# Partition sums with bfloat16 ones, norms of x moved beside projections, and the last sum of x split, in a kernel that mixes a memory attention and a gated feed-forward

## The chip, the cores and the metric

The kernel runs on one core of a Trainium2 chip. The metric is the device time of one execution in microseconds. Engines are named as in the profile: PE is TensorE (PEld its weight loads), DVE is VectorE, ACT is ScalarE, POOL is GpSimd, SP is SyncE, which here issues the DMAs.

## The reference, cut to what matters

With S = 2048 tokens, D = 576, 32 heads of 18, F = 4608, and the tokens in N = 4 segments of L = 512:

```python
g = sigmoid((x * gate_w).sum(-1, keepdims=True))
q, k, v = x @ wq, x @ wk, x @ wv          # split in 32 heads and 4 segments
for s in range(4):                        # M, z: memory of the segments before
    p = softmax(q[s] @ k[s].T * scale + causal mask)
    a_dot = p @ v[s]
    a_mem = (phi(q[s]) @ M) / (phi(q[s]) @ z + 1e-6)
    o[s] = gb * a_mem + (1 - gb) * a_dot  # gb = sigmoid(beta), one for each head
    M += phi(k[s]).T @ v[s]; z += phi(k[s]).sum()
a = o @ wo
b = (gelu(x @ w_gate) * (x @ w_up)) @ w_down
return g * a + (1 - g) * b
```

`phi(t)` is t + 1 for t > 0, and exp(t) otherwise. All arrays are float32.

## The kernel before

Every large product is made in float16 pairs: a float32 operand is scaled by a power of two and split into a high and a low float16 word, and three products (high by high, high by low, low by high) are added in PSUM. The scales come from norms. A norm is a sum of squares, made along the free dimension by ACT or DVE into a column of `wst` or `stat`, and then over the 128 partitions by `sums` (L88): a product of a 128x128 matrix of ones with the few columns (3 to 10), whose result every partition holds. Only the exponent of the result is kept (`root`, `scale_of`, `scales`), so a scale is a power of two.

The work stands in an order written out by hand: inside `tc.manual_schedule` each of PE, ACT, DVE and POOL executes its instructions in the order in which the Python code issues them. An instruction that has to wait holds up all that stands behind it on its engine. PSUM has eight banks, given out by tag: `st` and `dn` (two each), `G`, `U`, `V` and `pv`. A new use of a bank waits until its last readers are done. `spare()` hands out `dn` or `V` in turns.

The stages:

- Segments s = 0 to 3 of 512 tokens. For s > 0, first the rows, q = 0 to 3: values for 128 tokens (`vrows`), transposes of the key rows of the segment before (`key_rows`, into G or st, and the last two into V), their product into the memory (`memorize`) and reads of the memory (`recall`). Then the projections j = 0 to 8 (`project`), each 14 products of 512 columns; a block of 128 columns of q or k goes to `put_columns`, which ACT and DVE work on: first words and an exponential on ACT, and later (`later`, `finish_later`) phi and the second words on DVE, an addition on POOL. What else belongs beside a projection is issued by `beside_products`, what belongs beside rows by `beside_rows` and `behind_rows`. The next segment's x is loaded, squared (`square_x`), added up over its five parts (`add_squares`) and split in words (`high_x`, `low_x`) beside the projections of the one before.
- `norm_x(c, o)` takes the added squares of segment c and multiplies them by ones over the partitions, 512 columns into bank V; DVE then takes the largest column as a bound for the hidden scales (`x2`). `NORMS` says where: beside the rows (1, 1), (1, 3), (2, 3) and (3, 0), ahead of `key_rows`.
- The feed-forward, `step(v)` for v = 0 to 71, two steps for each of 36 blocks of 128 hidden columns; a step handles two segments by Strassen-like sums of x and of the weights (`product`, `rest`, banks V, G, U). From the fifth step on a head of the attention is worked on beside it (`scores`, `powers`, `pair_rows`, `turn_rows`, `values`, `normalize`), and the product with `w_down` of the blocks before (`chains`, `down`, into banks dn by turns, added up by DVE at L1112). `scales` is called once in every four steps.
- `last_sum(p, i)` forms the last of the sums of two segments' x. For p = 1 it has three parts: a subtraction on POOL (i = 0, in segment 3), a copy that makes the high words on ACT, and a subtraction on DVE that makes the low words; the latter two with i = 1 in step 0, behind the first copy of G into U. Its result, the words of `x16[3]`, is first read in step 1.
- At the end the product with `wo`, and the stores.

Of the kernel before, what the change touches and what calls it, by code (L numbers as in the profile page):

```python
# [8 lines left out]
F32 = mybir.dt.float32  # L9
BF16 = mybir.dt.bfloat16  # L10
F16 = mybir.dt.float16
I32 = mybir.dt.int32
AF = mybir.ActivationFunctionType
# [5 lines left out]
P = 128  # L19
# [24 lines left out]
def kernel(ctx: ExitStack, tc: tile.TileContext, xs, wqk, wv, wo, wgu, wd, beta, out):  # L44
    nc = tc.nc
    pe, act, dve, pool, sp = nc.tensor, nc.scalar, nc.vector, nc.gpsimd, nc.sync

    cst = ctx.enter_context(tc.tile_pool(name="cst", bufs=1))
# [4 lines left out]
    def bank(tag, bufs=1, dt=F32):  # L53
        return ps.tile([P, 512 if dt == F32 else 1024], dt, name=tag, tag=tag, bufs=bufs)
# [11 lines left out]
    def flat(ap):  # L66
        return ap.rearrange("p a b -> p (a b)") if len(ap.shape) == 3 else ap
# [20 lines left out]
    def sums(st, o=None):  # L88

        o = (spare() if o is None else o)[:, : st.shape[1]]  # L90
        pe.matmul(o, ones, st, start=True, stop=True)
        return o

    def scale_of(i, total):
# [67 lines left out]
    def norm_x(c, o):  # L162
        pe.matmul(o, onesb, x_sq.pop(c)[:, :L], start=True, stop=True)
        n = x2[:, c : c + 1]
        dve.tensor_reduce(n, o, AX.X, OP.max)
        dve.tensor_scalar(n, n, 1e-30, None, OP.max)
# [209 lines left out]
    def last_sum(p, i):  # L376
        r, x, sc = sums_x[p], x16[2 * p + 1], xsc[:, 2 * p : 2 * p + 1]
        if i == 0:
            pool.tensor_tensor(r[2, 1], r[2, 1], r[2, 2], OP.subtract)
            return  # L380
        act.activation(flat(x[:, 0:2]), r[2, 1], AF.Copy, scale=sc)
        dve.scalar_tensor_tensor(flat(x[:, 4:6]), r[2, 1], sc, flat(x[:, 0:2]), OP.mult, OP.subtract)

    qks, vps, oms, oas = [], [], [], []
# [3 lines left out]
        oms.append(dram.tile([HT, D], F32, name="om"))  # L388
        oas.append(dram.tile([HT, 9 * P], F16, name="oa"))

    ones = cst.tile([P, P], F32, name="ones")
    onesb = cst.tile([P, P], BF16, name="onesb")
    mask = cst.tile([P, L], BF16, name="mask")
    gh = cst.tile([P, 2, H], F32, name="gh")
# [17 lines left out]
    with tc.tile_pool(name="prj", bufs=2, side="right", reuse_waits="tile") as pp:  # L412
# [44 lines left out]
        def make_v(k):  # L457
            t = W[9 + k] = pa.tile([P, 2, D + 2], F16, name="wv", bufs=5)
            pair_of(t, raw_v[:, k], wsc[:, 1:2])
# [201 lines left out]

        FIRST = (0,)
        with tc.manual_schedule(engines=ORDERED):
            pool.memset(onesb, 1.0)
            pool.memset(ones, 1.0)

            start = bank("G")
            for _ in range(30):
# [116 lines left out]
            def beside_products(s, j):  # L785
                if s < 3 and j == (4 if s else 5):
                    scale_x(s + 1, bank("V") if s == 0 else None)
                if s == 0:
                    if j == 0:
                        put_rows(0, 0, 0, va[0], usc, 1.0)  # L790
                        make_qk(3, pair_high)
                        finish_later()
                        make_qk(3, pair_low)
                    if j == 1:
                        scale_sum(0, wst[:, 10:19], va[3][:, 420:])
                        turns.update(of=3, n=4)
                        dve.tensor_scalar(unq, wis[:, 4:5], 2.0**-14, wsc[:, 0:1], OP.mult, OP.mult)
                        outscale(0, 0)
                        outscale(0, 2)
                        put_rows(0, 1, 0, va[1], usc, 1.0)  # L800
                        finish_later()
                    if j == 2:
                        make_qk(4)
                        make_v(1)
                        for q in (2, 3):
                            put_rows(0, q, 0, va[q], usc, 1.0)
                        for q in FIRST:
                            put_rows(0, q, 1, vb[q], usc, 1.0)
                        finish_later()
                        x_raw.pop(0)  # L810
                    if j == 3:
                        outscale(0, 1)
                    if j == 1 or 3 <= j < 6:
                        make_v(j - 1)
                if s == 1:
                    if j == 2:
                        dve.tensor_scalar(gh[:, 1], gh[:, 1], 1.0, None, OP.add)
                        dve.reciprocal(gh[:, 0], gh[:, 1])
                        dve.tensor_scalar(gh[:, 1], gh[:, 0], -1.0, 1.0, OP.mult, OP.add)
                    if j == 5:  # L820
                        for c in range(3):
                            mix_scale(c)
                if s < 3:
                    next_x(s + 1, j)
                if s == 2:
                    if j == 0:
                        form_sums(0, 2, 1)
                        last_sum(0, 0)
                    if j == 1:
                        last_sum(0, 1)  # L830
                    if j == 3:
                        load_sums(1)
                    if j == 8:
                        for f in range(3):
                            load_g(f)
                if s == 3:
                    if j == 0:
                        sums_g(0)
                        last_sum(1, 0)
                    if j == 1:  # L840
                        high_g(0, 1)
                        low_g(0, 1)
                    if j == 2:
                        load_d(0)
                        load_d(1)
                    if j == 4:
                        load_g(3)
                    if j == 6:
                        high_g(1, 0)
                        low_g(1, 0)  # L850
                        sums_g(1)
                        squares(1, 2, 0)
                        squares(1, 2, 1)
                    if j == 7:
                        squares(1, 3, 0, act_square)
                        squares(1, 0, 2, act_square)
                    if j == 8:
                        high_g(1, 1)
                        low_g(1, 1)
                        squares(1, 3, 1, act_square)  # L860
                        squares(1, 1, 2, act_square)
                    if 1 <= j < 4:
                        form_sums(1, j - 1, 2)
                    if 2 <= j < 5:
                        form_sums(1, j - 2, 1)

            NORMS = {(1, 1): (0,), (1, 3): (1,), (2, 3): (2,), (3, 0): (3,)}
            done = None
            for s in range(4):
                p = s - 1  # L870
                if s:
                    for q in range(4):
                        pv = vrows(s, q, 0)
                        if q == 0:
                            key_scale(p)
                        if done:
                            put_columns(*done)
                            done = None
                        finish_later()
                        put_rows(s, q, 0, *pv)  # L880
                        for c in NORMS.get((s, q), ()):
                            norm_x(c, bank("V"))
                        if q:
                            key_rows(p, q - 1)
                        beside_rows(s, q)
                        finish_later()
                        if held:
                            held.pop()()
                        behind_rows(s, q)
                        pv = vrows(s, q, 1)  # L890
                        put_rows(s, q, 1, *pv)
                        if p >= 1:
                            recall(p, q)
                        if q:
                            memorize(p, q - 1)
                    finish_later()
                    key_rows(p, 3)
                for j in range(9):
# [32 lines left out]
                    if s == 0 and j >= 6:  # L931
                        q = j - 5
# [20 lines left out]
    with tc.tile_pool(name="keep", bufs=2, side="right", reuse_waits="tile") as kp, ExitStack() as tail:  # L953
# [179 lines left out]
        def gelu(f, c, o, t):  # L1133
            act.activation(t, o, AF.Gelu_apprx_tanh, scale=scl[f // 2][0][:, 2 + c : 3 + c])  # L1134
# [94 lines left out]
        def step(v):  # L1229

            f, p = divmod(v, 2)
            fb, i4 = divmod(v, 4)
            c, e = 2 * p, 2 * p + 1
# [15 lines left out]
            V, g1 = ahead.pop(v) if v in ahead else first_product(v)  # L1249
# [1 line left out]
            product(X, f, A11, x1, 0, 4, True)  # L1251
            put(2 * k - 1, 3)
            dve.tensor_copy(Y, X)
            if v == 0:
                last_sum(1, 1)
            if v == 1:
                scale_result()
            if v != 4:
# [31 lines left out]
            if not fb:  # L1290
                dve.tensor_tensor(g0, V, g0, OP.add)
                gelu(f, c, g0, g0)
            some(fb - 1, early[0 if v == 4 else 1 : 2])
            if v == 2 * NF - 1:
                finish(2)
# [18 lines left out]
            put(2 * k, 1)  # L1314
            dve.tensor_tensor(g1, Y, g1, OP.add)  # L1315
            gelu(f, e, g1, g1)
            if v == 3:
                for n in range(2):
                    high_d(n)
                    low_d(n)  # L1320
# [303 lines left out]
```

## Time and profile before

| | |
|---|---|
| median of 3 runs | 1573.54 us (1573.29 to 1574.6) |
| profiled execution, own time | 1574.6 us |
| its span, first to last instruction | 1572.9 us |
| granted TensorE clock, mean | 0.999 |
| busy: PE, DVE, ACT, POOL | 1563.1, 1150.6, 1174.8, 1232.8 us |
| DMA | 209.90 MB, 133 GB/s |

A busy time is the sum of an engine's instructions; PE's matmuls are pipelined, so that one's duration runs on beside the start of the next. In the order of time a row is a start, a duration, engine, line, operation, output and inputs with their shapes, a count of merged instructions, and in brackets the idle time ahead of it with what ended it.

### The profile page before, as it was taken

How to read it: one execution, taken by the hardware profiler on the slowest of the kernel's cores; microseconds unless marked ns; L12 is line 12 of the kernel's file. 1: busy time of each engine (PE TensorE's matmuls, PEld its weight loads, DVE VectorE, ACT ScalarE, POOL GpSimd, SP SyncE). 2: the span in 40 equal slices, each digit the busy share in tenths (PEclk: the TensorE clock that was granted, in tenths of full speed). 3: DMA queues.
4: the chain of work that ended last, by engine and by line, in shares of the span. 5: the costliest groups of instructions: out<-in, count | busy, mean ns of one | idle time of the engine just before them, and what ended most of it. 6: DMA issues, size and time to landing. Idle time of an engine off the chain costs nothing.

```text
span 1572.9 us, 32770 instructions
## 1 busy us (share of the span) xinstructions
PE 1563.1 (99%) x11920; PEld 927.9 (59%) x11920; DVE 1150.6 (73%) x3027; ACT 1174.8 (75%) x1999; POOL 1232.8 (78%) x1184
## 2 busy tenths in 40 slices
PE   9999999999999999999999999999999999999998
PEld 5665754555555555555555555555555555555576
DVE  6788975767777776767777777777676777776565
ACT  7566544988788888878888878888887888885421
POOL 4354765888888879898888888887979788888697
PEclk9999999999999999999999999999999999999999
DMA  6633332688888799988888889888798978784644
GB/s 233 211 125 112 136 122 69 118 125 128 136 132 142 123 151 128 139 127 137 130 128 131 136 133 140 138 129 155 127 134 137 137 135 130 130 132 83 142 107 130
DMA packets 472826, 209.90 MB, mean 133 GB/s; under 512 B 427688, under 2 KB 437416, under 8 KB 472152
## 3 DMA queue, kind: packets, MB, share of 16 engines
q1 hardware_dynamic: 472664, 207.80, 73.4%
q8 instruction: 94, 1.54, 0.4%
q14 instruction: 68, 0.56, 0.1%
HBM read 91.87 MB, written 27.26 MB: 76 GB/s over the span
## 4 chain that ended last, share of the span: by engine, by line
PE 94%; ACT 2%; DVE 1%; POOL 1%; issue 1%; DMA 0%; SPq 0%; POOLq 0%; ACTq 0%; DVEq 0%
PE dn L1104 27%; PE U L1144 18%; PE V L1144 12%; PE G L1144 12%; PE pv L1059 4%; PE dn L342 2%; PE st L335 2%; PE U L1151 2%; PE V L1156 1%; PE G L1156 1%; PE st L1012 1%; PE st L1464 1%; PE V L1151 1%; PE G L1151 1%; PE G L335 1%; PE U L335 1%
## 5 line engine op out<-in xcount | busy, mean ns | idle before, releaser
L1039 POOL TENSOR_TENSOR ph<-pf,ph 128x512 f16<-128x512 f32 (+1 forms) x256 | 353.8, 1404 | 173.0 <-ACT ph L1038 173.0
L1104 PE MATMUL dn<-paird,hh 128*128 128x288 f16 x3396 | 476.5, 286 | 0.2 <-DVE acc L1112 0.2
L1144 PEld LDWEIGHTS <-pairg 128*128 128x128 f16 x3024 | 284.8, 98 | 305.3 <-issue 18.7
L1104 PEld LDWEIGHTS <-hh 128*128 128x128 f16 x3456 | 331.2, 97 | 154.6 <-issue 18.5
L1112 DVE SCALAR_TENSOR_TENSOR acc<-dn,ev,acc 128x288 f32<-128x288 f32 x534 | 274.3, 515 | 53.7 <-PE dn L1104 43.7
L1028 ACT ACTIVATE pf<-pf,mb,esc 128x512 f32<-128x512 f32 (+3 forms) x512 | 292.9, 642 | 6.7
L1144 PE MATMUL U<-xt,pairg 128*128 128x512 f16 x864 | 210.0, 379 | 0.0
L1144 PE MATMUL G<-x,pairg 128*128 128x512 f16 x864 | 210.0, 379 | 0.0
L1131 POOL TENSOR_TENSOR hh<-gl,hh 128x512 f16<-128x512 f32 x144 | 164.5, 1163 | 19.1 <-ACT hh L1130 19.1
L316 POOL TENSOR_TENSOR pairg<-raw,pairg 128x640 f16<-128x640 f32 (+2 forms) x144 | 175.6, 1241 | 4.3 <-ACT pairg L312 4.3
L312 ACT ACTIVATE pairg<-raw 128x640 f16<-128x640 f32 (+2 forms) x144 | 90.0, 650 | 114.9 <-POOL raw L306 66.6
L1289 DVE COPY gl<-U 128x512 f32<-128x512 f32 x72 | 49.8, 692 | 168.1 <-POOL hh L1131 151.2
L1038 ACT ACTIVATE ph<-pf 128x512 f16<-128x512 f32 (+1 forms) x256 | 172.4, 720 | 0.0
L1015 DVE CUSTOM_DVE_ANT_0 pf<-st,mask 128x512 f32<-128x512 f32 (+1 forms) x256 | 157.2, 614 | 0.0
L281 POOL TENSOR_SCALAR raw<-raw,sc 128x640 f32<-128x640 f32 x72 | 135.9, 1900 | 0.0
L1015 DVE CUSTOM_DVE_ANT_0 pf<-dn,mask 128x256 f32<-128x256 f32 (+1 forms) x192 | 67.2, 375 | 81.5 <-PE dn L1012 81.2
L1134 ACT ACTIVATE gl<-gl,sc 128x512 f32<-128x512 f32 x144 | 96.6, 715 | 37.0 <-DVE gl L1315 19.3
L1144 PE MATMUL V<-xt,pairg 128*128 128x512 f16 x432 | 105.7, 381 | 0.0
L1144 PE MATMUL V<-x,pairg 128*128 128x512 f16 x432 | 104.8, 378 | 0.4 <-DVE gl L1212 0.4
L1144 PE MATMUL U<-x,pairg 128*128 128x512 f16 x432 | 105.0, 379 | 0.0
L1130 ACT ACTIVATE hh<-gl 128x512 f16<-128x512 f32 x144 | 82.6, 616 | 15.8 <-DVE gl L1126 15.7
L1059 PEld LDWEIGHTS <-pt 128*128 128x128 f16 x2560 | 83.4, 96 | 6.4
(312 smaller groups left out, 2651.7 us busy)
## 6 DMA issues: line engine op xcount, KB each, us to landing
raw<-in_wgu_dram SPq DMA_DIRECT2D x36, 640.0 KB
rawd<-in_wd_dram SPq DMA_DIRECT2D x36, 288.0 KB
qt<-qk SPq DMA_DIRECT2D x132, 72.0 KB
kt<-qk SPq DMA_DIRECT2D x132, 72.0 KB
qk<-stage SPq DMA_DIRECT2D x36, 256.0 KB
qt<-qk SPq DMA_DIRECT2D x132, 36.0 KB
kt<-qk SPq DMA_DIRECT2D x132, 36.0 KB
vp<-vstage SPq DMA_DIRECT2D x16, 296.0 KB
```

The source lines that it names most:

```text
L281: pool.tensor_scalar(r, r, scl[f // 2][0][:, 0:1], None, OP.mult)
L316: pool.tensor_tensor(spot(f, *p, 1), raw_g[f][:, p[0] : p[1]], spot(f, *p, 0), OP.subtract)
L1015: dve.tensor_tensor_reduce(prob[a][:, COL[qi] : COL[qi + 1]], out[qi], mask[:, L - (qi + 1) * P :], 1.0, -3e38, OP.add, OP.max, mx[a][:, q ...
L1028: act.activation(r, r, AF.Exp, bias=b[:, qi : qi + 1], scale=esc[:, 0, c : c + 1])
L1038: act.activation(h[:, 0, cols], p[:, cols], AF.Copy)
L1039: pool.tensor_tensor(h[:, 1, cols], p[:, cols], h[:, 0, cols], OP.subtract)
L1059: pe.matmul(ov, pr[:, 10 * i + COL[qi] // P + kb], v[:, 4 * e + kb, c0 : c0 + VC], start=kb == 0 and i == 0, stop=kb == qi and i == 1)
L1104: pe.matmul(o[:, :NH], hh[:, a, q * P : (q + 1) * P], w[:, b, n * NH : (n + 1) * NH], start=i == 0, stop=i == 5)
L1112: dve.scalar_tensor_tensor(av, o[:, :NH], ev, av, OP.mult, OP.add)
L1131: pool.tensor_tensor(hh[:, 1], t, hh[:, 0], OP.subtract)
L1134: act.activation(t, o, AF.Gelu_apprx_tanh, scale=scl[f // 2][0][:, 2 + c : 3 + c])
L1144: pe.matmul(o, w[:, i, (a + k) * P : (a + k + 1) * P], x[:, b + k], start=start and k == 0 and i == 0 and b == h, stop=k == 1 and i == 1, ...
```

## The change

Three edits. `sums` multiplies bfloat16 ones by the upper halves of the float32 words of its columns, which are read as bfloat16 with a step of two; the matrix of float32 ones and its memset go, and the bfloat16 ones become 1 + 2^-6, which also `norm_x` uses. The norms of segments 0, 1 and 2 are issued from `beside_products`, at the projections (1, 1), (1, 5) and (2, 5); that of segment 3 stays at the rows (3, 0). `last_sum(1, 1)` in step 0 is split: the copy on ACT is issued behind the first gelu, the subtraction on DVE behind the second one; `last_sum(0, 1)` makes both at once as before.

```diff
--- before.py
+++ after.py
@@ -88,7 +88,7 @@
     def sums(st, o=None):
 
         o = (spare() if o is None else o)[:, : st.shape[1]]
-        pe.matmul(o, ones, st, start=True, stop=True)
+        pe.matmul(o, onesb, st.bitcast(BF16).rearrange("p (n h) -> p n h", h=2)[:, :, 1], start=True, stop=True)
         return o
 
     def scale_of(i, total):
@@ -378,7 +378,10 @@
         if i == 0:
             pool.tensor_tensor(r[2, 1], r[2, 1], r[2, 2], OP.subtract)
             return
-        act.activation(flat(x[:, 0:2]), r[2, 1], AF.Copy, scale=sc)
+        if i == 1:
+            act.activation(flat(x[:, 0:2]), r[2, 1], AF.Copy, scale=sc)
+            if p:
+                return
         dve.scalar_tensor_tensor(flat(x[:, 4:6]), r[2, 1], sc, flat(x[:, 0:2]), OP.mult, OP.subtract)
 
     qks, vps, oms, oas = [], [], [], []
@@ -388,7 +391,6 @@
         oms.append(dram.tile([HT, D], F32, name="om"))
         oas.append(dram.tile([HT, 9 * P], F16, name="oa"))
 
-    ones = cst.tile([P, P], F32, name="ones")
     onesb = cst.tile([P, P], BF16, name="onesb")
     mask = cst.tile([P, L], BF16, name="mask")
     gh = cst.tile([P, 2, H], F32, name="gh")
@@ -661,8 +663,7 @@
 
         FIRST = (0,)
         with tc.manual_schedule(engines=ORDERED):
-            pool.memset(onesb, 1.0)
-            pool.memset(ones, 1.0)
+            pool.memset(onesb, 1.0 + 2.0**-6)
 
             start = bank("G")
             for _ in range(30):
@@ -812,6 +813,8 @@
                         outscale(0, 1)
                     if j == 1 or 3 <= j < 6:
                         make_v(j - 1)
+                if (s, j) in NORMS:
+                    norm_x(NORMS[s, j], bank("V"))
                 if s == 1:
                     if j == 2:
                         dve.tensor_scalar(gh[:, 1], gh[:, 1], 1.0, None, OP.add)
@@ -864,7 +867,7 @@
                     if 2 <= j < 5:
                         form_sums(1, j - 2, 1)
 
-            NORMS = {(1, 1): (0,), (1, 3): (1,), (2, 3): (2,), (3, 0): (3,)}
+            NORMS = {(1, 1): 0, (1, 5): 1, (2, 5): 2}
             done = None
             for s in range(4):
                 p = s - 1
@@ -878,8 +881,8 @@
                             done = None
                         finish_later()
                         put_rows(s, q, 0, *pv)
-                        for c in NORMS.get((s, q), ()):
-                            norm_x(c, bank("V"))
+                        if s == 3 and q == 0:
+                            norm_x(3, bank("V"))
                         if q:
                             key_rows(p, q - 1)
                         beside_rows(s, q)
@@ -1251,8 +1254,6 @@
             product(X, f, A11, x1, 0, 4, True)
             put(2 * k - 1, 3)
             dve.tensor_copy(Y, X)
-            if v == 0:
-                last_sum(1, 1)
             if v == 1:
                 scale_result()
             if v != 4:
@@ -1290,6 +1291,8 @@
             if not fb:
                 dve.tensor_tensor(g0, V, g0, OP.add)
                 gelu(f, c, g0, g0)
+                if v == 0:
+                    last_sum(1, 1)
             some(fb - 1, early[0 if v == 4 else 1 : 2])
             if v == 2 * NF - 1:
                 finish(2)
@@ -1314,6 +1317,8 @@
             put(2 * k, 1)
             dve.tensor_tensor(g1, Y, g1, OP.add)
             gelu(f, e, g1, g1)
+            if v == 0:
+                last_sum(1, 2)
             if v == 3:
                 for n in range(2):
                     high_d(n)
```

## The prediction

> **What bounds the kernel now.** I read the page first, for the span and the chain that ended last, then the busy times by stage, then TensorE's list of waits, and at the end the order of time around each place that the change touches.
>
> ```profile
> span 1572.9 us, 32770 instructions
> ...
> PE 94%; ACT 2%; DVE 1%; POOL 1%; issue 1%; DMA 0%; SPq 0%; POOLq 0%; ACTq 0%; DVEq 0%
> ```
>
> Nearly the whole chain is TensorE's, so what it issues and what it waits for is the time. The busy times by stage (columns: stretch and its length, then busy time and count for PE, PEld, DVE, ACT and POOL, granted clock, DMA share, GB/s):
>
> ```profile
> 54.00:74.00 20.00, 19.31 (x178) 15.89 (x176) 13.29 (x37) 7.79 (x18) 6.47 (x9) 1.00 0.55 185
> ...
> 286.00:1450.00 1164.00, 1164.00 (x9336) 676.80 (x9333) 860.62 (x2385) 971.66 (x1624) 983.67 (x901) 1.00 0.84 133
> ```
>
> From 286 to 1450 us TensorE is busy for every one of 1164 us, and no other engine is above 984: each nanosecond less on TensorE there shortens the kernel, and no other engine is near enough to become the bound for a tenth of a microsecond per block. The rows of the second segment, 54 to 74 us, lack 0.69 us. Who made TensorE wait there, from the list of waits (total, times, longest):
>
> ```profile
> PE st L91 <- ACT krow L442: 1.4, 1, 1.4
> PE V L602 <- DVE x L165: 1.0, 3, 0.3
> ```
>
> L165 is the reduction of a norm of x, L602 the transposes of the key rows into the same bank V: three times, as many as there are norms ahead of transposes. The change touches exactly these waits, and the sums on the stretch that is all TensorE.
>
> **Part 1, sums over partitions.** Every call of `sums` was one float32 product, which the trace shows as two passes:
>
> ```profile
> L91 PE MATMUL dn<-stat,ones x38: 173/218/258, 162.9 to 1451.4; 128*128 128x10 f32 x38
> ...
> L91 PE MATMUL st<-wst,ones x4: 245/253/274, 11.5 to 17.3; 128*128 128x5 f32 x2, 128*128 128x4 f32 x2
> ...
> L91 PE MATMUL pv<-wst,ones x4: 168/213/257, 18.9 to 26.0; 128*128 128x5 f32 x2, 128*128 128x9 f32 x2
> ...
> L91 PE MATMUL V<-wst,ones x4: 169/212/254, 38.6 to 143.5; 128*128 128x5 f32 x4
> ...
> L91 PE MATMUL dn<-wst,ones x4: 169/211/253, 90.1 to 1484.9; 128*128 128x5 f32 x2, 128*128 128x3 f32 x2
> ```
>
> 54 passes are 27 calls. Matmuls are pipelined, so a call's price is not its duration but the step from its start to the next matmul's start (order of time, TensorE alone; start, duration, tile, count):
>
> ```profile
> 1451.35 0.29 PE L91 MATMUL dn<-stat,ones 128*128 128x10 f32 x2
> 1451.49 1.46 PE L1144 MATMUL G<-x,pairg 128*128 128x512 f16 x6
> ...
> 295.95 0.66 PE L1059 MATMUL pv<-vt,pt 128*128 128x37 f16 x20
> 296.46 0.81 PE L1144 MATMUL V<-x,pairg 128*128 128x512 f16 x3
> ```
>
> Before: 1451.49 - 1451.35 = 0.14 us for two passes. After there is one load of 128x128 16-bit weights and one pass of 3 to 10 columns. Its nearest row is the products of probabilities and values: 20 pairs of a 128x128 16-bit load and a 37-column pass take 296.46 - 295.95 = 0.51 us, 0.0255 each, the step to the next 512-column product included. So a call saves 0.14 - 0.0255 = 0.114 us. That the words are read two bytes out of four touches only these few columns. 19 calls (38 passes into dn, 162.9 to 1451.4), two into V and two into dn from 38.6 us on stand where TensorE runs without a gap: 23 x 0.114 = 2.6 us. The four calls before 26.1 us lie in the start, which waits for loads and scales; I take nothing for them, and 4 x 0.114 = 0.5 us as the other end. The weights' factor 1 + 2^-6 and the shortened words change values, not work; one memset less on POOL lies beside the first loads.
>
> The lower end of this term is the case in which the next weights can't be loaded beside so short a pass:
>
> ```profile
> 803.44 0.66 PE L1059 MATMUL pv<-vt,pt 128*128 128x37 f16 x20
> ...
> 804.03 0.39 PE L1156 MATMUL G<-x,pairg 64*128 64x512 f16 x1
> ```
>
> Here the same 20 pairs take 0.59 us up to a product on 64 rows: with 19 steps of 0.0255 the last one is 0.11 us. With 0.11 instead of 0.0255 a call saves 0.03 and the 23 save 0.7 us. That row changes the number of array rows; the sum, its neighbours before and behind all use 128, as in the row at 296.46, so I take 0.0255. The Trainium skill (TensorE: Matmul & The Clock Gate, section Back-to-back issue gap) speaks against this: it gives about 81 ns for each pair of load and matmul in a stream at 128 columns, and warns that short passes are undercounted. By that price, an estimate from that page, a call would save 0.06 us and the part 1.4 us. This trace's pairs at 0.0255 us disagree with it, and the measured row decides.
>
> **Part 2, norms beside projections.** Place by place (TensorE, with the reduction of DVE):
>
> ```profile
> 58.30 0.38 PE L163 MATMUL V<-pairg,onesb 128*128 128x512 bf16 x1
> 58.51 0.60 PE L600 MATMUL st<-ident,phi 128*128 128x128 f32 x4
> ...
> 58.71 0.69 DVE L165 TENSOR_REDUCE x<-V 128x1 f32<-128x512 f32 x1 [0.68 <-PE V L163]
> ...
> 59.46 0.44 PE L602 MATMUL V<-ident,phi 128*128 128x128 f32 x2 [0.35 <-DVE x L165]
> 59.51 0.45 DVE L540 SCALAR_TENSOR_TENSOR vstage<-U,vstage 128x288 f16<-128x288 f32 x1
> 59.73 0.53 PE L342 MATMUL dn<-wv,x 128*128 128x290 f16 x3
> ...
> 64.13 0.60 PE L600 MATMUL st<-ident,phi 128*128 128x128 f32 x4
> ...
> 64.79 0.41 PE L342 MATMUL dn<-wv,x 128*128 128x290 f16 x2
> ```
>
> The norm's product fills V, four transposes go elsewhere, and the two that need V again wait until DVE has reduced it. From the first transpose to the next row product it is 59.73 - 58.51 = 1.22 us; with no norm ahead, 64.79 - 64.13 = 0.66. So 0.56 us each, three times: 1.7 us. In the changed order the norms of x stand behind the projections (1,1), (1,5) and (2,5), where no transposes follow and no projection uses V; the product itself (0.21 us, 58.30 to 58.51) is issued as before. The fourth norm keeps its place.
>
> What it adds is a wait on DVE's queue. There the reduction now stands ahead of the later half of put_columns of the block before (phi and the low words), and waits for a projection that TensorE is still working on. The tightest place is (2,5):
>
> ```profile
> 143.57 6.20 PE L335 MATMUL st<-x,wp 128*128 128x512 f16 x28
> 149.61 3.19 PE L335 MATMUL U<-x,wp 128*128 128x512 f16 x14
> 152.63 3.19 PE L335 MATMUL G<-x,wp 128*128 128x512 f16 x14
> ...
> 146.02 0.74 DVE L514 TENSOR_SCALAR phi<-G,al 128x512 f32<-128x512 f32 x1
> ...
> 154.13 1.46 DVE L193 SCALAR_TENSOR_TENSOR x<-raw,xsc,x 64x512 f16<-64x512 f32 x1
> ...
> 157.12 0.29 PE L344 MATMUL dn<-wv,x 128*128 128x288 f16 x1
> ```
>
> Two projections take 149.61 - 143.57 = 6.04 us, so the first ends at 146.59, or 146.48 with the sum before it 0.11 shorter. The reduction starts 0.41 us after its product (58.71 - 58.30) and the next operation 0.80 after that (59.51 - 58.71): 147.69. The phi of bank G, at 146.02 before, comes 1.67 us late. DVE has next to no idle time up to the last low words of x, which end at 154.13 + 1.46 = 155.59, so at worst at 157.26. Who waits for them is L344 at 157.12, now 0.10 later (norm 0.21 more, sum 0.11 less): 157.22. So the slack of 1.5 us is just used up. Queued behind are the phi additions on POOL and the release of bank G, which the projection after next needs only at 152.63. I take 0 for this, and 0.2 us, or 1.7 us if DVE slips further, as the other end; a gain is excluded, since nothing waited there. At (1,1) and (1,5) the same working leaves more room.
>
> **Part 3, the last sum of x.** `last_sum(1, 1)` put a copy on ACT ahead of the last stage copy, and a subtraction on DVE behind the first copy into U:
>
> ```profile
> 212.36 1.13 ACT L381 ACTIVATE x<-acc,xsc 128x1024 f16<-128x1024 f32 x1
> ...
> 213.40 0.57 ACT L504 ACTIVATE stage<-G 128x512 f16<-128x512 f32 x1
> ...
> 214.01 0.69 DVE L520 SCALAR_TENSOR_TENSOR stage<-G,stage 128x512 f16<-128x512 f32 x1 [0.62 <-ACT stage L504]
> ...
> 215.82 0.68 DVE L1212 COPY gl<-V 128x512 f32<-128x512 f32 x1
> ...
> 216.56 1.46 PE L1144 MATMUL V<-x,pairg 128*128 128x512 f16 x6 [0.35 <-DVE gl L1212]
> ...
> 217.75 1.27 DVE L382 SCALAR_TENSOR_TENSOR x<-acc,xsc,x 128x1024 f16<-128x1024 f32 x1
> ...
> 223.98 0.74 DVE L1126 SCALAR_TENSOR_TENSOR gl<-G,sc,gl 128x512 f32<-128x512 f32 x1
> ...
> 226.19 1.46 PE L1144 MATMUL G<-x,pairg 128*128 128x512 f16 x6
> ```
>
> With the copy gone from there, ACT's stage copy of G comes about 1 us sooner, so DVE no longer idles 0.62 us for it. DVE is then busy without a gap up to the copy of V at 215.82, for which TensorE waits at 216.56: all move 0.62 us, to 215.20 and 215.94. TensorE's own pace allows hardly less, so I take the gain as 0.6 us, ends 0 and 0.7. The copy and the subtraction return behind the gelus of the first step, 1.27 us of DVE ahead of the operation at 223.98, which then ends near 223.98 + 1.27 + 0.74 = 225.99; TensorE writes G again at 226.19. So 0.2 us of cover is left; if gone, it costs up to the missing part. No DMA moves in any part.
>
> **The sum.** 2.6 + 1.7 + 0.6 = 4.9 us. The profiled execution took 1574.6 us with a span of 1572.9 (1.7 around it), so the span should be 1568.0. That execution is the slowest of three; the median is 1573.54, so I forecast 1568.6 us.
>
> **Rivals.** First, the short pass exposes the next weights: part 1 gives 0.7 instead of 2.6, the total is 3.0 and the time 1570.5. For it speaks the step of 0.11 us at 804.03, against it the row at 296.46. Chance 0.12, for any part of this exposure. By the estimate from the Trainium skill's page (81 ns a pair, see part 1) it would be 3.7 us in all and 1569.8.
>
> Second, DVE slips: the low words of x come too late at one or both row starts, and 1.7 us are given back: 3.2 us in all, 1570.3. For it speaks that DVE has no gap there, against it the room worked out above. Chance 0.10.
>
> Third, slower: the sum now has a weight load of its own, and in the changed order this load carries the wait for a bank dn. Should it be held by DVE's addition for the chain right before it, the load and all behind it stand still. That addition in the block of the call at 1451.35:
>
> ```profile
> 1451.55 0.52 DVE L1112 SCALAR_TENSOR_TENSOR acc<-dn,ev,acc 128x288 f32<-128x288 f32 x1
> ```
>
> It ends 0.72 us after the sum's start (1451.55 + 0.52 - 1451.35). All but the first two of the 19 calls have such a chain ahead of them; 17 x 0.72 = 12.2 us lost against the 4.9 gained give 1580.9. The point from which it decides against no change is 4.9 / 17 = 0.29 us a call. Against it: the chain and the sum take the two banks dn in turn, and the list of waits has L91 in one row alone, into st in the start. Chance 0.04.
>
> The remaining 0.74 is my forecast.
>
> About 0.2%, 3.1 us, is what a measurement of this kernel can tell from no change: 1570.4. The forecast lies beyond it, the first two rivals around it. Faster 0.80, same 0.15, slower 0.05. The range reaches from 1567.4 (0.5 for the first four sums, and 0.7 for run-to-run scatter) to 1571.2, past both small rivals.
>
> **What would show it.** Right: L91 with 27 passes in all and a step of 0.03 us to the next product; the row "V L602 <- DVE x L165" gone from the waits, and the transposes to row product at 0.66 us in all blocks; the copy of V 0.6 us sooner against the last projection, and TensorE's wait for it near zero. Wrong: a step of 0.1 us behind L91, a wait of L344 for DVE at the third or fourth segment's first rows, a wait of G's product at the second step for L1126, or any wait of L91 itself.

## The result and the profile after

The changed kernel takes 1569.67 us (median of 9 runs, 1568.78 to 1570.42) beside 1574.17 us for the kernel before (9 runs on the same chip, 1573.29 to 1575.5): a ratio of 0.9972 with an interval of 0.9962 to 0.9982, so 4.5 us less, by the interval 2.8 to 6.0. The profiled execution took 1570.42 us with a span of 1568.6; the forecast for it was 1568.0, and 1568.6 for the median. Line numbers have moved by 1 to 5 (L602 is now L604, L1104 L1107, L1144 L1147, L1469 L1474).

The page of the changed kernel, with the span and the chain that ended last:

```profile
span 1568.6 us, 32692 instructions
...
PE 87%; DVE 4%; ACT 3%; DMA 3%; POOL 2%; issue 1%; SPq 0%; DVEq 0%; ACTq 0%
```

TensorE's share of the chain fell from 94 to 87%: the walk back now leaves TensorE more often, which is a first sign that somewhere it arrives sooner than its inputs. (In the runs below it is 88% with the sums alone, and 96% where POOL's memset is moved.) The stages of the prediction (stretch, length, then busy time of PE, PEld, DVE, ACT, POOL, clock, DMA share, GB/s):

```profile
54.00:74.00 20.00, 20.00 (x183) 16.42 (x182) 12.85 (x35) 8.54 (x20) 6.40 (x9) 1.00 0.52 188
286.00:1450.00 1164.00, 1163.54 (x9321) 676.50 (x9320) 860.91 (x2388) 971.78 (x1625) 983.50 (x902) 1.00 0.82 132
```

The second segment's rows have no idle time any more (19.31 of 20 us were busy before), but the long stretch, without a gap before, now lacks 0.46 us. The waits of TensorE:

```profile
PE st L91 <- ACT krow L444: 2.2, 1, 2.2
PE G L670 <- POOL onesb L666: 1.0, 1, 1.0
PE st L335 <- DVE wp L112: 0.3, 1, 0.3
PE dn L342 <- DVE gate L544: 0.2, 1, 0.2
PE U L625 <- DVE krow L612: 0.2, 1, 0.2
```

The transposes' wait for L165 is gone, and so is that of the product into V for the copy L1215. New are L342 and L625, both at the rows of the last segment. The wait of L91 in the start is 0.8 longer, because TensorE comes there earlier; the sum itself starts at 17.30 us, and started at 17.14.

**The three edits at their places.** The sums, in all and at one call (order of time, TensorE; start, duration, tile, shapes, count):

```profile
L91 PE MATMUL dn<-stat,onesb x19: 170/171/171, 160.8 to 1448.4; 128*128 128x10 bf16 x19
...
1448.44 0.17 PE L91 MATMUL dn<-stat,onesb 128*128 128x10 bf16 x1
1448.46 1.46 PE L1147 MATMUL G<-x,pairg 128*128 128x512 f16 x6
```

One pass each, and 1448.46 - 1448.44 = 0.02 us to the next product, where it was 0.14. Over the calls from 38.6 us on, without the one at 160.77, the mean step is 0.028 us, where it was 0.140: 0.112 less a call (0.114 was forecast).

The rows behind the norm's old place:

```profile
58.23 0.60 PE L602 MATMUL st<-ident,phi 128*128 128x128 f32 x4
...
58.66 0.38 PE L604 MATMUL V<-ident,phi 128*128 128x128 f32 x2
...
58.88 1.65 PE L342 MATMUL dn<-wv,x 128*128 128x290 f16 x12
```

From the first transpose to the next row product it is 58.88 - 58.23 = 0.65 us instead of 1.22.

The split last sum (DVE and TensorE):

```profile
212.15 0.68 DVE L522 SCALAR_TENSOR_TENSOR stage<-G,stage 128x512 f16<-128x512 f32 x1
...
213.95 0.68 DVE L1215 COPY gl<-V 128x512 f32<-128x512 f32 x1
...
214.72 1.46 PE L1147 MATMUL V<-x,pairg 128*128 128x512 f16 x6
...
223.23 0.74 DVE L1129 SCALAR_TENSOR_TENSOR gl<-G,sc,gl 128x512 f32<-128x512 f32 x1
...
224.25 1.46 PE L1147 MATMUL G<-x,pairg 128*128 128x512 f16 x6
```

DVE no longer idles ahead of L522, the product into V no longer waits, and behind the returned subtraction L1129 ends at 223.97, 0.28 us ahead of TensorE's next use of G.

**Where it does not arrive.** I set the start of every matmul against the same one before. The last product of the program starts at 1564.57 instead of 1567.77, 3.20 us sooner; the rest of the span's 4.3 us lies behind it:

```profile
1564.57 0.41 PE L1474 MATMUL st<-wo,ot 128*128 128x288 f16 x2
```

From there to the span's end it is 5.1 us before and 4.0 after. A second profile of the kernel before (e8 below) has 3.9, so these 1.1 us are scatter of the end and not the change. The first sums, in the start, gain nothing that lasts (0.06 us at 43.5 us). From there to the last product the profile has 3.14 us, where the three parts amount to 4.8 (22 of the sums at 0.112, 2.46; norms 1.7; last sum 0.67). The missing part sits in two places. At the rows of the last segment, 161 to 166 us, TensorE gives back 0.94 us, and the 0.11 of the sum there isn't seen, 1.05 in all. And in seven of the blocks of four steps that have one sum each, at 354 to 796 us, the sum's 0.11 is given back some 4.5 us later, at the first product into `dn` behind the scores: 7 x 0.118 = 0.8 us.

The first place, in the kernel before (SP, ACT and TensorE):

```profile
152.98 0.34 SPq L213 DMA_DIRECT2D raw<-in_wgu_dram  x1
...
158.60 0.73 ACT L442 ACTIVATE krow<-raw 128x640 bf16<-128x640 f32 x1
...
163.03 1.64 PE L342 MATMUL dn<-wv,x 128*128 128x290 f16 x12
```

And in the changed kernel (DVE, SP, ACT and TensorE in order of time):

```profile
144.67 0.69 DVE L165 TENSOR_REDUCE x<-V 128x1 f32<-128x512 f32 x1 [0.87 <-PE V L163]
...
149.91 2.00 DVE L188 SCALAR_TENSOR_TENSOR x<-raw,xsc,x 128x1024 f16<-128x1024 f32 x1
...
151.94 0.35 SPq L213 DMA_DIRECT2D raw<-in_wgu_dram  x1
...
157.92 0.74 ACT L444 ACTIVATE krow<-raw 128x640 bf16<-128x640 f32 x1 [1.34 <-DMA raw<-in_wgu_dram]
...
161.16 1.66 PE L342 MATMUL dn<-wv,x 128*128 128x290 f16 x12 [0.23 <-DVE gate L544]
...
164.93 0.68 PE L625 MATMUL U<-vstage,krow 128*128 128x152 f16 x7 [0.20 <-DVE krow L612]
```

DVE waits 0.87 us for the moved norm. The low words of x end at 151.91 and free their `raw` buffer, and SP issues the load of feed-forward weights into it at 151.94. Before, it was issued at 152.98; TensorE is 2.12 us earlier there, the load only 1.04. The load lands at 157.9, 6.0 us later, and ACT stands 1.34 us in its squares, with the copies of values and the key rows queued behind. They come late, and TensorE waits for their banks and words.

The second place, in the block whose sum starts at 352.69 us (354.76 before); first the kernel before (DVE, TensorE), then the changed one (POOL, DVE, TensorE):

```profile
358.80 0.51 DVE L1112 SCALAR_TENSOR_TENSOR acc<-dn,ev,acc 128x288 f32<-128x288 f32 x1
...
359.19 0.21 PE L1012 MATMUL pv<-kt,qt 54*128 54x128 f16 x1
359.36 0.89 PE L1104 MATMUL dn<-paird,hh 128*128 128x288 f16 x6
```

```profile
351.01 0.34 POOL L997 MEMSET ob<- 128x288 f32 x1
351.31 2.27 POOL L1134 TENSOR_TENSOR hh<-gl,hh 128x512 f16<-128x512 f32 x2
...
352.51 0.69 DVE L1290 COPY gl<-U 128x512 f32<-128x512 f32 x1 [2.64 <-POOL hh L1134]
...
356.73 0.51 DVE L1115 SCALAR_TENSOR_TENSOR acc<-dn,ev,acc 128x288 f32<-128x288 f32 x1
...
357.02 0.21 PE L1015 MATMUL pv<-kt,qt 54*128 54x128 f16 x1
357.29 1.63 PE L1107 MATMUL dn<-paird,hh 128*128 128x288 f16 x12
```

DVE's addition, which frees the bank, ends at 357.24, and TensorE's product starts at 357.29, 0.27 us behind the scores instead of 0.17. DVE has no gap from 352.51 on; there it waited for POOL, whose words of the hidden columns stand behind a memset. That memset stands in the seven blocks that hand back, and once more at 280.7 us before (278.8 after), where nothing is handed back. No row in the list of waits tells of these tenths: they show only in the steps.

### The profile page after: what moved, and what is told of

Read it like the earlier page. It is cut to its first block, busy times and chain, and to the rows that moved or that the text cites. A ratio compares the mean times of both kernels' runs of the same rounds, so it can differ in the third digit from the quotient of the medians.

```text
span 1568.6 us, 32692 instructions
## 1 busy us (share of the span) xinstructions
PE 1560.4 (99%) x11893; PEld 926.2 (59%) x11893; DVE 1151.0 (73%) x3027; ACT 1174.4 (75%) x1999; POOL 1229.9 (78%) x1183
## 4 chain that ended last, share of the span: by engine, by line
PE 87%; DVE 4%; ACT 3%; DMA 3%; POOL 2%; issue 1%; SPq 0%; DVEq 0%; ACTq 0%
PE dn L1107 25%; PE U L1147 16%; PE V L1147 11%; PE G L1147 10%; PE pv L1062 4%; PE st L335 2%; PE dn L342 2%; PE U L1154 2%; POOL ph L1042 1%; PE V L1159 1%; PE st L1015 1%; PE G L1159 1%; PE G L335 1%; PE U L335 1%; PE st L1469 1%; DMA orow<-oa 1%
## 5 line engine op out<-in xcount | busy, mean ns | idle before, releaser
L1107 PE MATMUL dn<-paird,hh 128*128 128x288 f16 x3396 | 476.6, 287 | 0.6
L1147 PEld LDWEIGHTS <-pairg 128*128 128x128 f16 x3024 | 283.7, 98 | 304.8 <-issue 18.0
L1107 PEld LDWEIGHTS <-hh 128*128 128x128 f16 x3456 | 332.4, 98 | 154.1 <-issue 18.3
L1147 PE MATMUL U<-xt,pairg 128*128 128x512 f16 x864 | 210.0, 380 | 0.0
L1147 PE MATMUL G<-x,pairg 128*128 128x512 f16 x864 | 210.0, 379 | 0.0
L1147 PE MATMUL V<-xt,pairg 128*128 128x512 f16 x432 | 105.8, 381 | 0.0
L1147 PE MATMUL U<-x,pairg 128*128 128x512 f16 x432 | 105.0, 380 | 0.0
L1147 PE MATMUL V<-x,pairg 128*128 128x512 f16 x432 | 104.8, 378 | 0.0
```

What stands on the lines that cost most here:

```text
L1107: pe.matmul(o[:, :NH], hh[:, a, q * P : (q + 1) * P], w[:, b, n * NH : (n + 1) * NH], start=i == 0, stop=i == 5)
L1147: pe.matmul(o, w[:, i, (a + k) * P : (a + k + 1) * P], x[:, b + k], start=start and k == 0 and i == 0 and b == h, stop=k == 1 and i == 1, ...
```

## The experiments

The ratios are set against the kernel before on the same chip, the paths against its first profile. Since differences of tenths of a microsecond are asked for, the path of TensorE is read beside the times: the start of its last product, and that of one early row product (L345, 43.52 us in the kernel before), because the start itself scatters (see the end). The gain on the path is the first difference less the second.

| run | ratio to before, interval | L345 at | last product at | gain on the path |
|---|---|---|---|---|
| before, first profile | | 43.52 | 1567.77 | |
| changed, first profile | 0.9972 [0.9962, 0.9982] | 43.45 | 1564.57 | 3.1 |
| sums alone | 0.9983 [0.9973, 0.9992] | 43.24 | 1566.02 | 1.5 |
| norms alone | 0.9985 [0.9976, 0.9995] | 43.77 | 1566.10 | 1.9 |
| last sum alone | 0.9993 [0.9984, 1.0003] | 44.67 | 1568.08 | 0.8 |
| norm at (2, 2) | 0.9970 [0.9958, 0.9982] | 43.36 | 1563.88 | 3.7 |
| memset moved | 0.9968 [0.9956, 0.9980] | 44.03 | 1563.89 | 4.4 |
| both | 0.9970 [0.9959, 0.9982] | 43.94 | 1563.45 | 4.7 |
| changed, second profile | | 43.35 | 1563.98 | 3.6 |
| before, second profile | | 44.64 | 1569.04 | -0.15 |

From 1479 to 1510 us, near the end of the feed-forward, single profiles scatter by up to 0.3 us either way. Read at 1479 us, ahead of that, the gain is 1.53 with the sums alone, 1.66 with the norms alone, 0.65 with the last sum alone, 2.96 and 3.37 in the two profiles of the changed kernel, 3.99 with the norm at (2, 2), 4.43 with the memset moved and 4.93 with both.

### The sums alone

```diff
-        pe.matmul(o, ones, st, start=True, stop=True)
+        pe.matmul(o, onesb, st.bitcast(BF16).rearrange("p (n h) -> p n h", h=2)[:, :, 1], start=True, stop=True)
...
-    ones = cst.tile([P, P], F32, name="ones")
...
-            pool.memset(onesb, 1.0)
-            pool.memset(ones, 1.0)
+            pool.memset(onesb, 1.0 + 2.0**-6)
```

> The kernel before with the first edit alone: sums by bfloat16 ones. Read by the start of the last product on TensorE (1567.77 us before, 1564.57 in the changed kernel), since the end behind it moves by itself. Theory A, the prediction: 23 calls keep 0.11 us each, the last product starts at 1565.2, the median falls by 2.6 us. Theory B, from the changed kernel's trace: seven of the blocks (about 350 to 870 us) hand their 0.11 us back 4.6 us behind the sum, since a bank dn is held by a DVE chain that POOL starts; then 1566.0, median down by 1.8 us, and no wait at the fourth segment's rows.

Measured: 1571.61 us beside 1573.68, and the last product at 1566.02, theory B's number (1566.0; theory A had 1565.2); 0.28 us of that comes from the start, and on the path the gain is 1.5. The medians lie 2.1 apart, between the two theories (2.6 and 1.8). Every call from 38.6 us on saves 0.11, and the same seven blocks hand 0.11 to 0.14 back. So that loss belongs to this edit alone. The rows of the last segment lose nothing here:

```profile
162.39 0.17 PE L91 MATMUL dn<-stat,onesb 128*128 128x10 bf16 x1
162.41 1.64 PE L342 MATMUL dn<-wv,x 128*128 128x290 f16 x12
```

### The norms alone

```diff
+                if (s, j) in NORMS:
+                    norm_x(NORMS[s, j], bank("V"))
...
-            NORMS = {(1, 1): (0,), (1, 3): (1,), (2, 3): (2,), (3, 0): (3,)}
+            NORMS = {(1, 1): 0, (1, 5): 1, (2, 5): 2}
...
-                        for c in NORMS.get((s, q), ()):
-                            norm_x(c, bank("V"))
+                        if s == 3 and q == 0:
+                            norm_x(3, bank("V"))
```

> The kernel before with the second edit alone: three norms of x beside the projections (1, 1), (1, 5), (2, 5). Theory A: 0.56 us for each, the last product starts at 1566.1. Theory B: the norm at (2, 5) holds DVE, the low words of the next x come late, the weight loads that need their buffers start late, ACT waits for one of them ahead of a value copy, and TensorE gives back about 1 us at the fourth segment's rows: 1567.1, with a wait of ACT for raw<-in_wgu. If that wait does not appear here, it belongs to the sum of the edits (loads that come no sooner while the work does).

Measured: 1571.94 us, and the last product at 1566.10: 1.9 us on the path, of which 3 x 0.57 = 1.70 at the three places, and 0.12 at 125.8 us, where a wait for key rows goes with the norm. That is theory A's last product (1566.1). The late load of theory B is there, but ACT hardly feels it:

```profile
152.49 0.34 SPq L213 DMA_DIRECT2D raw<-in_wgu_dram  x1
...
157.60 0.74 ACT L442 ACTIVATE krow<-raw 128x640 bf16<-128x640 f32 x1 [0.47 <-DMA raw<-in_wgu_dram]
```

It lands 5.1 us after its issue, not 6.0, and TensorE gives back 0.08 + 0.05 us. So the norm at (2, 5) takes away the slack of this load, and how much is lost hangs on the length of the load's flight and on how far TensorE's and ACT's work has moved forward meanwhile.

### The last sum alone

```diff
-        act.activation(flat(x[:, 0:2]), r[2, 1], AF.Copy, scale=sc)
+        if i == 1:
+            act.activation(flat(x[:, 0:2]), r[2, 1], AF.Copy, scale=sc)
+            if p:
+                return
...
-            if v == 0:
-                last_sum(1, 1)
...
+                if v == 0:
+                    last_sum(1, 1)
...
+            if v == 0:
+                last_sum(1, 2)
```

> The kernel before with the third edit alone: the last sum of x split behind the gelus. Both theories: 0.6 us, the last product starts at 1567.1, and TensorE's wait at the start of the feed-forward for the copy of V is gone. Theory B adds that nothing of it is handed back later, since the blocks' hand-back is bound to the place of the sum in each block: at most 0.1 us.

Measured: 1572.62 us; the ratio's interval holds 1, so the times alone can't tell this edit from none. On the path it is plain: 0.15 us at the product into G and 0.51 at the one into V (0.27 more at 1500 us, near the end of the feed-forward, where the two profiles of one and the same kernel differ by 0.2 too). The last product is late, at 1568.08, only because this execution lost 1.15 us in the start.

```profile
216.28 0.69 DVE L1215 COPY gl<-V 128x512 f32<-128x512 f32 x1
...
217.05 1.46 PE L1147 MATMUL V<-x,pairg 128*128 128x512 f16 x6
```

### The changed kernel with the third norm at (2, 2)

```diff
-            NORMS = {(1, 1): 0, (1, 5): 1, (2, 5): 2}
+            NORMS = {(1, 1): 0, (1, 5): 1, (2, 2): 2}
```

> The changed kernel with the norm of segment 2 at the projection (2, 2) instead of (2, 5), where DVE has idle time ahead of it. Theory A: nothing changes, last product at 1564.6. Theory B: the low words of x come as early against TensorE as in the kernel before, ACT's wait for the weights and TensorE's waits at 161 to 165 us are gone, about 1 us gained: 1563.6.

Measured: 1569.35 us, 3.7 us on the path. The norm is now three projections away from the low words that free the buffer (SP, ACT, TensorE):

```profile
150.79 0.34 SPq L213 DMA_DIRECT2D raw<-in_wgu_dram  x1
...
156.39 0.72 ACT L444 ACTIVATE krow<-raw 128x640 bf16<-128x640 f32 x1
...
160.68 0.17 PE L91 MATMUL dn<-stat,onesb 128*128 128x10 bf16 x1
160.71 1.64 PE L342 MATMUL dn<-wv,x 128*128 128x290 f16 x12
```

The load is issued 1.15 us sooner, ACT does not wait, and the step behind the sum is 0.03 us, where it was 0.39. The whole loss of the first place is gone; the seven blocks still hand back theirs. Against the second profile of the changed kernel (below) the lead is 0.72 us at 170 us and 0.62 at 1479; at the last product only 0.1 of it is left, a change within the scatter of the stretch between. This shows the chain: norm, DVE's queue, buffer, load, ACT, bank.

### The changed kernel with POOL's memset elsewhere

```diff
-            if t0:
-                pool.memset(o[:, :t0], 0.0)
...
+        def zero_memory(gg):
+            if gg < H // 4:
+                pool.memset(obs[gg][:, :4], 0.0)
...
+                if k % 4 == 1:
+                    zero_memory(k // 4)
```

The memset of `ob`, which only the heads of the first 1024 tokens need, moves on, from ahead of POOL's words of the hidden columns to a place behind them.

> The changed kernel with POOL's zeroing of the output rows of the first half's heads issued one step later, ahead of the lower words of the probabilities instead of ahead of the lower words of the hidden values. Theory B (the bank dn is held by a DVE chain that starts when POOL has freed a buffer, and the zeroing, 0.34 us in the first half alone, is what makes POOL late there): the step of 0.28 us from the scores to the first product into dn falls to 0.15 to 0.17, the seven blocks keep their 0.11 us, 0.8 us gained on TensorE. Rival: the hand-back comes from the scales themselves, DVE's eight small operations behind the sum; then nothing changes.

Measured: 1568.55 us, 4.4 us on the path. All seven blocks keep their 0.11 (POOL, DVE, TensorE in the same block):

```profile
351.05 2.28 POOL L1136 TENSOR_TENSOR hh<-gl,hh 128x512 f16<-128x512 f32 x2
...
352.25 0.69 DVE L1294 COPY gl<-U 128x512 f32<-128x512 f32 x1 [2.37 <-POOL hh L1136]
...
356.47 0.51 DVE L1117 SCALAR_TENSOR_TENSOR acc<-dn,ev,acc 128x288 f32<-128x288 f32 x1
...
357.03 0.21 PE L1017 MATMUL pv<-kt,qt 54*128 54x128 f16 x1
357.18 1.64 PE L1109 MATMUL dn<-paird,hh 128*128 128x288 f16 x12
```

DVE's wait for POOL falls from 2.64 to 2.37, the addition ends 0.26 us sooner, and TensorE's step behind the scores is 0.15 instead of 0.27. The rival, DVE's small operations behind the sum, is out: they stand there unchanged, and the hand-back is gone. In this execution the rows of the last segment lose 0.5 us, the sum's 0.11 in it (ACT waits 0.78 for the load).

### Both

> The changed kernel with the norm of segment 2 at (2, 2) and the zeroing moved. If both hand-backs are what they were taken for, the last product starts at 1563.0 or earlier (1563.88 with the norm moved alone), and the median is about 1 us below that of the norm moved alone. If the two share a cause, no lower than 1563.9.

```diff
-            NORMS = {(1, 1): 0, (1, 5): 1, (2, 5): 2}
+            NORMS = {(1, 1): 0, (1, 5): 1, (2, 2): 2}
...
+                if k % 4 == 1:
+                    zero_memory(k // 4)
```

Measured: 1568.83 us; 4.7 us on the path, where the three parts amount to 4.8 from 43.5 us on.

```profile
1563.45 0.41 PE L1478 MATMUL st<-wo,ot 128*128 128x288 f16 x2
```

The last product starts at 1563.45, between the two bounds of the expectation; 0.42 us of that is the start, and on the path the gain over the norm moved alone is 1.0. The expected 1 us between the medians did not show: 4.7 us below the kernel before here, 4.3 there. The whole runs can't tell this version from the changed kernel: the intervals of the last four ratios overlap almost wholly. The path says 1.1 to 1.6 us better; the medians, each against the kernel before on its own chip, 4.7 beside 4.5.

### Both kernels once more

The changed kernel and the kernel before, unchanged, with a new profile each, for the scatter of single profiles.

> The changed kernel once more, for a second profile. If the rows of the fourth segment are held by the load of weights, ACT's wait for raw<-in_wgu is there again, but its length follows how long that load takes (5.9 us in the first profile, 5.1 us in the kernel with the norms alone), and TensorE's loss at 161 to 165 us follows it (0 to 1 us). The time from the last product's start to the end of the span (4.0 us in the first profile, 5.1 us in that of the kernel before) moves by up to 1 us between executions.

> The kernel before once more, for a second profile: the same steps on TensorE between 26 us and the last product to within 0.1 us; from the last product to the end of the span 4.0 to 5.1 us, if that difference is scatter and not the change's.

Measured: 1569.77 and 1574.74 us, spans of 1568.0 and 1572.9. The second profile of the changed kernel gives 3.6 us on the path, with the same seven blocks handing back, and 0.7 us lost at the last segment's rows, the sum's 0.11 in it (ACT waits 0.99). The second profile of the kernel before keeps within 0.05 us of the first from 43.5 to 1479 us, and then differs by 0.17. So a path is known to some 0.2 us where nothing waits, and the loss at the last segment's rows, the sum's 0.11 in it, varies between 0.5 and 1.05.

## Why the prediction was right, and which steps were off

**The price of a sum held.** 0.112 us saved against 0.114. The first rival, a step of 0.11 that exposes the next weights, did not happen: 25 of the 27 calls have a step of 0.03 us or less, and the weight loads of L91 take 0.10 us and lie beside the product ahead. The other two calls wait for something else: the one at 18.88 us (0.13) for the next product's weights, which ACT makes at L716, and the one at 160.77 for a bank. By the figure of the Trainium skill (TensorE: Matmul & The Clock Gate, section Back-to-back issue gap: about 81 ns for each pair in a stream at 128 columns) a call would have saved 0.06 us, an estimate; with passes of 10 columns this trace has 0.02 to 0.03, so the figure for 128 columns does not carry over to them.

**Part 1's sum was too large.** The step that multiplies 0.114 by all 23 calls, since they "stand where TensorE runs without a gap", took a TensorE without gaps for one that no other engine paces. In the blocks at 354 to 796 us DVE released the bank just as TensorE came to it (359.31 beside 359.36 before, 357.24 beside 357.29 after; TensorE's start is 4.60 us behind the sum's in both), so the cover of other work there was already nil. The chain that ends in this release begins ahead of the sum (POOL's memset at 351.01, the sum at 352.69), so a shorter sum does not move it. About 1.6 us of the 2.6 were kept in the changed kernel: seven blocks returned 0.8, the sum at 160.77 brought nothing, and all those ahead of 43.5 us left 0.06. The prediction read busy times to say that no other engine could become the bound; that says nothing of an engine that is late once in a block.

**Part 2 held, and its zero did not.** 3 x 0.57 = 1.70 against 3 x 0.56, and 0.12 at 125.8 us that was not foreseen. The reduction came 0.42 us after its product (0.41 was taken), and DVE's low words came late, though less than the 1.67 us worked out for the worst case: the load behind them by 1.08 us against TensorE. What failed is the sentence "I take 0 for this", and beside it "No DMA moves in any part". The prediction asked who reads the low words, found L344, and found just enough room; L344 never waited. It didn't ask who takes the buffer that they read. That is a load, with 5 to 6 us of flight and ACT at its end, and it cost 0.94 and 0.6 us in the two profiles of the changed kernel, besides the 0.11 of the sum there. This is the second rival's cause, DVE's slip at (2, 5), at another place and at about half its price.

**Part 3 held.** 0.67 us against 0.6, and the cover left behind the returned subtraction is 0.28 us against 0.2.

**The slower rival** did not happen: no wait of L91 for a bank, and a step of 0.03 us at all calls but the two named above.

**The total.** 4.9 us were forecast, and the whole runs say 4.5 (2.8 to 6.0). The path says 3.1 and 3.6 in two profiles. In the first pair of profiles another 1.1 us lie behind the last product, and those are scatter, as the second profile of the kernel before shows. A start that varies by a microsecond from one execution to the next is in the medians too. By the path 1.3 to 1.8 us of the 4.9 are missing, and yet the saving between the medians is within 0.4 us of the forecast: that is in part luck, and how much the scatter gave to it stays open. The path is the surer reading, and by it the forecast was some 1.5 us too hopeful.

## What to carry to other kernels

An engine that is busy all the time can still be paced by another once in every block: before you multiply a saving by the calls, look at the first bank or word behind each call, when its releaser ends and where that releaser's chain begins. When a step is moved on an engine's queue, list what it delays by the buffers that are read as well as by the results that are written, because a buffer's next user may be a load that starts late and lands late. And where an edit is worth less than the scatter of whole runs, the start of each matmul set against the same one before shows to a few hundredths where it gains and where it is given back.

## What the runs showed of the hardware

**The clock in the start.** In four of the ten profiled executions (one of the kernel before, three of variants) TensorE had half its clock for some 3 us from about 17 to 18 us on, behind the wait of L91 for ACT. The kernel before, first and second profile, from 18.0 to 20.5 us (columns as above; the granted clock is the third from the end):

```profile
18.00:20.50 2.50, 2.50 (x13) 1.38 (x11) 2.43 (x7) 2.12 (x5) 0.00 (x0) 1.00 0.05 13
```

```profile
18.00:20.50 2.50, 2.50 (x6) 1.68 (x6) 2.40 (x7) 2.05 (x5) 0.00 (x0) 0.50 0.05 11
```

The same kernel ran 13 matmuls in the one and 6 in the other, which made 1.12 us at 43.5 us; the three variants came there 0.4 to 1.15 us late. It does not go by the length of the wait alone: with 2.2 us of it the first profile of the changed kernel kept its clock, with 1.6 the second of the kernel before lost it. The Trainium skill (TensorE: Matmul & The Clock Gate, section What's actually happening) says that the gate judges by a window of about 3.4 us that runs free of the kernel's start, so that it varies from run to run; the length of the spell and its coming and going here agree with that, and no run here shows the window itself.

**A float32 product of few columns** is two passes and 0.140 us of TensorE; the same sum of 16-bit words with their own weight load is one pass and 0.028.

**The flight of one load varied.** The same load of 640 KB at the same place took 5.1 us from issue to the reader that waits for it with the norms alone, 5.4 with the memset moved, and 5.6 and 6.0 in two executions of the changed kernel. The loss behind it went the same way: 0.1, 0.5, 0.7 and 1.05 us. What makes the flight longer, no run here shows.
